# MLP and gate layers of a convolution-gated network as four interleaved 512-token lanes, with weight gradients as 22 PSUM jobs

## The chip, the cores and the metric

The kernel runs on 1 core of one Trainium2 chip. The metric is the device time of one execution in microseconds. One core has TensorE (PE, with a queue PEld for loading weights), VectorE (DVE), ScalarE (ACT), GpSimd (POOL) and SyncE (SP), which here only issues transfers; 16 DMA engines move data between DRAM, the on-chip memory SBUF and, through the engines, the accumulators in PSUM.

## What is computed

The reference is a forward pass of four residual layers over 2048 tokens of width 512, and all its gradients:

```python
def _A_ref(q, k, v, shift_k, ssm_k, ssm_D):      # gate layer
    kv = k_shift * v                             # k_shift: 4-tap causal shift convolution of k
    y = irfft(rfft(kv, 2 * S) * rfft(ssm_k, 2 * S))[:S] + kv * ssm_D
    return q * y
def _B_ref(x, w1, b1, w2, b2):                   # MLP, 512 -> 1376 -> 512
    return gelu(x @ w1 + b1) @ w2 + b2
x = A_q
x = x + _A_ref(_layernorm(x), A_k, A_v, A_shift_k, A_ssm_k, A_ssm_D)
x = x + _B_ref(_layernorm(x), B_w1, B_b1, B_w2, B_b2)
x = x + _A_ref(_layernorm(x), ...)               # the same weights again
x = x + _B_ref(_layernorm(x), ...)
_out, _vjp = jax.vjp(_f, A_q, ..., B_b2)
return (_out, *_vjp(grad_out))                   # x and ten gradients
```

Layers are numbered 0 and 2 (gate) and 1 and 3 (MLP). y is the same in both gate layers, so the convolution runs once forward and once backward.

## The kernel before

Tiles are 128 partitions wide: 2048 tokens are 16 token tiles, 512 features are 4 chunks, 1376 hidden features are 11 chunks, the last of them 96 wide. The program is a row of phases, each of which runs after the one ahead as far as its data and its memory allow.

`phase_conv_forward` does the transforms as matmuls; its last inverse matmuls are at L206, and y stays in SBUF. Then `load_weights` loads w1 (512 x 1376), w2 (1376 x 512) and the biases; w1 and w2 go through the ACT queue, b1 as single elements at L560 and L563 through SP.

`phase_forward` runs `a_layer_fwd` and `b_layer_fwd` twice. A gate layer takes LayerNorm statistics (L532, L534, a square root on ACT at L535), normalizes, multiplies with y and adds. An MLP layer normalizes all 16 token tiles (L625), transposes them on PE (L630, evicted at L631), and then, for each slice of 512 tokens and each of 11 chunks, multiplies with w1 into PSUM (L640), evicts with the bias (L643), and forms gelu and its derivative gp on pieces of 128 x 512: eight operations on DVE (L646 to L664) and two on ACT (L653, L659). gp is stored feature-major by POOL (L665). Four token tiles are then multiplied with w2 (L670); DVE and whichever engine is free add the residual and b2 (L673, L674); h is transposed on PE to token-major (L602, evicted at L604) and stored (L678).

`phase_backward` first transposes w1 and w2 on PE (`build_bwd_weights`, L716). `b_layer_bwd` transposes the gradient (L783), multiplies with w2T (L802), multiplies with gp (L804, which also sums the bias gradient), multiplies with w1T (L811), goes back through LayerNorm (L735 on) and stores gz token-major after PE transposes (L820). The weight gradients follow inside the same layer function. dW2 is formed in two groups of up to six PSUM accumulators; for each group all 16 token tiles of h are read again (L837) and multiplied (L839). dW1 has 12 accumulators in two groups, and reads gz (L865) and n (L867) again for each (L869). Layer 3's sums go to DRAM as 32-bit partials and are added to layer 1's. `a_layer_bwd` handles the gate layers.

`phase_conv_backward` begins at L967. It multiplies with PE at L994, loads kv and its transform matrix, and runs the same transforms again; its code is not touched by the change.

Each engine and each DMA queue executes its instructions in program order; a scheduler sets that order when the program is built, within the order of the phases.

## Time and profile before

| | us |
|---|---|
| runs | 1800.83, 1804.43, 1805.06 |
| median of the runs | 1804.43 |
| span of the profiled execution | 1812.6 |
| last inverse matmul of the forward convolution starts | 375.9 |
| last output matmul of the forward layers starts | 772.8 |
| last weight-gradient matmul starts | 1341.8 |

The profile is of one execution, whose span is 8.2 us over the median of the runs. Rows are quoted further down. A row of the timeline is one instruction: start, duration, engine, line of the program, operation, output and input tiles, shapes. A row of the windows gives each engine's busy time in a stretch of the span.

### The profile page before, as it was taken

The page shows a single profiled execution, that of the slowest core. Times are in us where ns is not written, and L with a number is a line of the kernel's source. Part 1 is how long each engine was busy: PE and PEld are TensorE (multiplying, and loading weights), DVE is VectorE, ACT ScalarE, POOL GpSimd, SP SyncE. Part 2 cuts the span into 40 slices and gives each one's busy share as a digit, 9 for nine tenths or more (in the row PEclk, how much of TensorE's full clock was granted, in tenths as well). Part 3 has the DMA queues.
Part 4 walks back from the last instruction along what each step waited for, and adds up shares of the span by engine and source line. Part 5 has one row for each costly group of instructions (what it writes and reads, how often), then busy time and mean ns, then how long its engine had stood idle before and what let it go on. Part 6 is the DMA issues. An engine that isn't in the chain of part 4 may idle for free.

```text
span 1812.6 us, 17191 instructions
## 1 busy us (share of the span) xinstructions
PE 1106.2 (61%) x5093; PEld 466.0 (26%) x5093; DVE 1148.1 (63%) x2935; ACT 670.2 (37%) x1122; POOL 335.1 (18%) x503
## 2 busy tenths in 40 slices
PE   4365950935777376749964669954656827642077
PEld 2022320412232132325521225411212302210033
DVE  8489716257999799926766007758213159999841
ACT  7433620138787777734314014301001302211321
POOL 0055200212222322200000000100000005554000
PEclk9687875965998599869987889988876958875588
DMA  5656474031212222263276754297875152121201
GB/s 49 233 184 203 157 285 172 0 79 71 77 72 103 84 75 75 88 205 126 91 251 196 232 176 138 94 189 219 273 221 204 47 221 70 58 61 43 62 14 47
DMA packets 128782, 237.64 MB, mean 131 GB/s; under 512 B 21919, under 2 KB 91579, under 8 KB 128048
## 3 DMA queue, kind: packets, MB, share of 16 engines
q1 hardware_dynamic: 81040, 117.24, 22.6%
q0 software_dynamic: 23168, 94.72, 13.8%
q10 hardware_dynamic: 24480, 24.58, 4.4%
q8 instruction: 40, 0.66, 0.2%
q14 instruction: 54, 0.44, 0.1%
HBM read 145.96 MB, written 90.52 MB: 130 GB/s over the span
## 4 chain that ended last, share of the span: by engine, by line
issue 46%; DVE 18%; DMA 13%; PE 11%; POOL 7%; SPq 3%; ACT 2%; another core or an unknown queue 1%; POOLq 0%; DVEq 0%; ACTq 0%
DMA dw_n<-n_d 4%; PE dw_ps L869 2%; DVE gwacc L1091 2%; DVE gk_tmp L1082 2%; POOL gp_d L665 2%; SPq L306 2%; DMA KVspec_d<-KVspec 2%; DMA kj<-in_A_k_dram 2%; PE fwd_psc L182 2%; PE fwd_pss L185 2%; DVE gk_acc L1083 1%; PE inv_A L198 1%; PE inv_A L200 1%; DMA out_dram<-gw_b 1%
## 5 line engine op out<-in xcount | busy, mean ns | idle before, releaser
L670 PE MATMUL o_ps<-w_sb,hT_sl 128*128 128x512 bf16 (+1 forms) x352 | 109.3, 415 | 62.8 <-DVE hT_sl L654 61.4
L869 PE MATMUL dw_ps<-gz_tm,dw_n 128*128 128x512 bf16 (+1 forms) x384 | 96.6, 399 | 75.8 <-DMA dw_n<-n_d 64.0
L839 PE MATMUL dw_ps<-g_bf,h_tm 128*128 128x512 bf16 (+1 forms) x352 | 101.3, 438 | 54.3 <-DMA h_tm<-htm_d 49.6
L640 PE MATMUL z_ps<-nT,w_sb 128*128 128x512 bf16 (+1 forms) x352 | 103.2, 417 | 10.0 <-ACT g_u L643 4.7
L802 PE MATMUL gh_ps<-gT,w2T 128*128 128x512 bf16 (+1 forms) x352 | 86.9, 384 | 2.0 <-DVE gzT_sl L804 2.0
L811 PE MATMUL gn_ps<-w1T,gzT_sl 128*128 128x512 bf16 (+1 forms) x352 | 83.6, 379 | 0.0
L665 POOL DMA_DIRECT2D gp_d<-g_gp x88 | 48.1, 547 | 162.6 <-DVE g_gp L664 138.0
L804 DVE SCALAR_TENSOR_TENSOR gzT_sl<-gh_ps,gp_sl 128x512 bf16<-128x512 f32 (+1 forms) x88 | 60.4, 689 | 25.6 <-PE gh_ps L802 25.3
L869 PEld LDWEIGHTS <-dw_n 128*128 128x128 bf16 x384 | 36.5, 106 | 136.0 <-DMA dw_n<-n_d 57.0
L670 PEld LDWEIGHTS <-hT_sl 128*128 128x128 bf16 (+1 forms) x352 | 35.7, 103 | 133.6 <-DVE hT_sl L654 97.1
L630 PE MATMUL tr_ps<-ident,b_n 128*128 128x128 bf16 x128 | 18.1, 291 | 80.9 <-ACT b_n L625 67.5
L1090 POOL TENSOR_TENSOR gw_prod<-sh_bf,k_t 128x512 bf16<-128x512 bf16 x48 | 58.9, 1228 | 43.9 <-DVE gwacc L1091 31.4
L653 ACT ACTIVATE g_s<-g_arg 128x512 bf16<-128x512 bf16 (+1 forms) x88 | 54.9, 625 | 31.8 <-DVE g_arg L651 31.3
L839 PEld LDWEIGHTS <-h_tm 128*128 128x128 bf16 (+1 forms) x352 | 35.9, 112 | 119.3 <-DMA h_tm<-htm_d 71.6
L198 PE MATMUL inv_A<-KVspec,Iblk 128*128 128x512 bf16 x64 | 25.5, 399 | 64.1 <-DVE KVspec L262 64.1
L659 ACT ACTIVATE g_oms<-g_s,onescol_f 128x512 bf16<-128x512 bf16 (+1 forms) x88 | 63.2, 720 | 2.2
L643 ACT ACTIVATE g_u<-z_ps,b1col 128x512 bf16<-128x512 f32 (+1 forms) x88 | 60.0, 683 | 7.6 <-DVE g_w L657 1.2
L1091 DVE TENSOR_TENSOR gwacc<-gwacc,gw_prod 128x512 f32<-128x512 f32 x64 | 60.8, 961 | 1.0 <-POOL gw_prod L1090 1.0
L747 ACT ACTIVATE lb_j<-agn 128x512 bf16<-128x512 bf16 x32 | 20.1, 627 | 111.3 <-DVE agn L898 92.0
L820 POOL DMA_DIRECT2D gztm_d<-gz_tmj x32 | 17.3, 541 | 235.3 <-ACT gz_tmj L604 231.0
L786 DVE TENSOR_TENSOR b2acc<-b2acc,b_ps 1x512 f32<-1x512 f32 x2 | 1.4, 675 | 93.5 <-PE b_ps L785 93.5
L1013 ACT ACTIVATE GYspec<-fwd_psc 128x512 bf16<-128x512 f32 x16 | 9.6, 598 | 136.0 <-PE fwd_psc L182 136.0
(300 smaller groups left out, 3004.3 us busy)
## 6 DMA issues: line engine op xcount, KB each, us to landing
h_tm<-htm_d SPq DMA_DIRECT2D x64, 344.0 KB, 4.2
gz_tm<-gztm_d SPq DMA_DIRECT2D x64, 344.0 KB, 3.9
htm_d<-h_tm POOLq DMA_DIRECT2D x32, 344.0 KB, 2.5
gztm_d<-gz_tmj POOLq DMA_DIRECT2D x32, 344.0 KB, 2.9
gp_d<-g_gp POOLq DMA_DIRECT2D x80, 128.0 KB, 2.1
gp_sl<-gp_d ACTq DMA_DIRECT2D x8, 1280.0 KB, 8.8
sst<-Hspec_d SPq DMA_DIRECT2D x64, 128.0 KB, 2.2
dw_n<-n_d SPq DMA_DIRECT2D x64, 128.0 KB, 3.7
```

Source lines behind the costliest of these rows:

```text
L640: nc.tensor.matmul(ps[0:fcs, :], lhsT=w.w1[:, dc, f0:f0 + fcs], rhs=nT[:, dc, cols], start=(dc == 0), stop=(dc == ND - 1))
L643: nc.scalar.activation(out=u[0:fcs], in_=ps[0:fcs], func=ACT.Identity, bias=w.b1col[0:fcs, c:c + 1], scale=1.0)
L659: nc.scalar.activation(out=oms[0:fcs], in_=sg[0:fcs], func=ACT.Identity, scale=-1.0, bias=consts.onescol_f[0:fcs, :])
L665: nc.gpsimd.dma_start(out=gp_dram[f0:f0 + fcs, cols], in_=gp[0:fcs])
L670: nc.tensor.matmul(ps2, lhsT=hT_sl[0:fcs, c, ti * P:(ti + 1) * P], rhs=w.w2[0:fcs, c, :], start=(c == 0), stop=(c == NFC - 1))
L802: nc.tensor.matmul(ps[0:fcs, :], lhsT=bw.w2T[:, dc, f0:f0 + fcs], rhs=gT[:, dc, cols], start=(dc == 0), stop=(dc == ND - 1))
L804: nc.vector.scalar_tensor_tensor(out=gzT_sl[0:fcs, c, :], in0=ps[0:fcs], scalar=1.0, in1=gp_sl[0:fcs, c, :], op0=ALU.mult, op1=ALU.mult, a ...
L811: nc.tensor.matmul(ps2, lhsT=gzT_sl[0:fcs, c, ti * P:(ti + 1) * P], rhs=bw.w1T[0:fcs, c, :], start=(c == 0), stop=(c == NFC - 1))
L839: nc.tensor.matmul(accs[c][0:fcs, :], lhsT=hm[:, f0:f0 + fcs], rhs=g_bf[:, t, :], start=(t == 0), stop=(t == NT - 1))
L869: nc.tensor.matmul(accs[(dc, fs0)][:, 0:fsz], lhsT=n_t[:, dc * P:(dc + 1) * P], rhs=gm[:, fs0:fs0 + fsz], start=(t == 0), stop=(t == NT - 1))
L1090: nc.gpsimd.tensor_tensor(out=prod, in0=sh[jj], in1=kt, op=ALU.mult)
L1091: nc.vector.tensor_tensor(out=gwacc[:, jj, :], in0=gwacc[:, jj, :], in1=prod, op=ALU.add)
```

## The change

The convolution phases stay. Everything between them is one new phase, `phase_mlp`.

The 2048 tokens are four lanes of 512. Each lane is a generator that walks through layers 0 to 3 (and in the backward pass 3 to 0) and yields estimated costs; `interleave` always resumes the lane whose clock is lowest, with the lanes started 12 (forward) or 8 (backward) units apart. A lane's x stays in SBUF as one 128 x 4 x 512 tile. LayerNorm's reciprocal root is a power on POOL. Transposes of n and of the gradients are DMA transposes (`turn`) instead of PE transposes. gelu runs on groups of up to four chunks, 128 x 2048: three ACT passes, two tensor_scalar and five tensor_tensor on DVE per group. Residual and b2 are added by PE as two more matmuls into the same accumulator, and ACT evicts. h, gp and gz are stored feature-major; the token-major copies are gone. All transfers of the phase are issued by SP.

In the backward pass the mean part of LayerNorm's gradient is taken out of w1T once, on DVE, when the weights are loaded (L551 to L553), and the other part is a matmul with a diagonal matrix built on POOL (L711, L713).

The weight gradients come after both layers: 22 jobs, 11 chunks of dW2 from h and 11 of dW1 from gz. A job brings in its chunk of both layers with two DMA transposes of 128 x 2048 (L779), multiplies 32 times into one accumulator (L784), and stores; dW1's results are transposed by DMA first (L792).

w1T and w2T are now made by DMA transposes from DRAM when the weights are loaded, before the forward pass (L541, L547). The last 96 columns of w1 come at L543: there the compiled program has, for each of the four row blocks, a plain transfer of 96 x 128 single elements.

The core of the diff, without the unchanged parts of formulas (removed functions are those shown above):

```diff
-    with tc.tile_pool(name="wsmall", bufs=1) as wsmall:
-        res.w = load_weights(nc, tc, wpool, wsmall, dims, aps)
-    phase_forward(nc, tc, dims, consts, dram, res, aps, dbg)
...
-    phase_backward(nc, tc, dims, consts, dram, res, aps, dbg)
+    with ExitStack() as res.gystack:
+        phase_mlp(nc, tc, dims, consts, dram, res, aps)
...
 def load_weights
+    w1_ap, w2_ap = aps["B_w1"], aps["B_w2"]
+    w.w1 = wpool.tile([P, ND, FP], BF16, name="w1_sb")
+    nc.sync.dma_start(out=w.w1[:, :, 0:F], in_=w1_ap.rearrange("(c p) f -> p c f", p=P))
...
+    for dc in range(ND):
+        rows = w1_ap[dc * P:(dc + 1) * P, :]
+        nc.sync.dma_start_transpose(out=w.w1T[:, 0:nfull, dc * P:(dc + 1) * P], in_=rows[:, 0:nfull * P])
+        if nfull < NFC:
+            nc.sync.dma_start_transpose(out=w.w1T[0:F - nfull * P, nfull, dc * P:(dc + 1) * P],
+                                        in_=rows[:, nfull * P:F])
+    for f0 in range(0, F, 512):
+        fsz = min(512, F - f0)
+        nc.sync.dma_start_transpose(out=w.w2T[:, :, f0:f0 + fsz], in_=w2_ap[f0:f0 + fsz, :])
...
+    for c in range(NFC):
+        st = small.tile([P, 6], F32, name="w1st", tag="w1st", bufs=3)
+        nc.vector.bn_stats(out=st, in_=w.w1T[:, c, :])
+        nc.vector.bn_aggr(out=mv[:, c, :], in_=st)
+        nc.vector.tensor_scalar(out=w.w1T[:, c, :], in0=w.w1T[:, c, :], scalar1=mv[:, c, 0:1], scalar2=None,
+                                op0=ALU.subtract)
...
 new functions
+def interleave(lanes):
+    clock = [off for off, _ in lanes]
+    gens = [g for _, g in lanes]
+    alive = set(range(len(gens)))
+    while alive:
+        i = min(alive, key=lambda k: (clock[k], k))
+        try:
+            clock[i] += next(gens[i])
+        except StopIteration:
+            alive.discard(i)
...
+def turn(nc, m, dst, src):
+    for t in range(TS):
+        nc.sync.dma_start_transpose(out=dst[:, :, t * P:(t + 1) * P], in_=src[:, t, :])
...
+    nc.scalar.activation(out=q, in_=zb, func=ACT.Square)
+    nc.vector.tensor_scalar(out=t, in0=q, scalar1=C_GELU2 * A_GELU, scalar2=C_GELU2, op0=ALU.mult, op1=ALU.add)
+    nc.vector.tensor_tensor(out=t, in0=t, in1=zb, op=ALU.mult)
+    nc.scalar.activation(out=sg, in_=t, func=ACT.Sigmoid)
+    nc.scalar.activation(out=o, in_=t, func=ACT.Sigmoid, scale=-1.0)
+    nc.vector.tensor_scalar(out=q, in0=q, scalar1=3.0 * C_GELU2 * A_GELU, scalar2=C_GELU2, op0=ALU.mult,
+                            op1=ALU.add)
+    nc.vector.tensor_tensor(out=h, in0=sg, in1=zb, op=ALU.mult)
+    nc.vector.tensor_tensor(out=o, in0=o, in1=h, op=ALU.mult)
+    nc.vector.tensor_tensor(out=o, in0=o, in1=q, op=ALU.mult)
+    nc.vector.tensor_tensor(out=gp, in0=o, in1=sg, op=ALU.add)
...
 b_fwd, per lane
+            nc.scalar.activation(out=zb[:, c - c0, :], in_=ps, func=ACT.Identity, bias=w.b1col[:, c:c + 1])
...
+        nc.sync.dma_start(out=m.h_d[l][:, c0:c0 + k, s * 512:(s + 1) * 512], in_=h[:, c0:c0 + k, :])
+        nc.sync.dma_start(out=m.gp_d[l][:, c0:c0 + k, s * 512:(s + 1) * 512], in_=gp[:, 0:k, :])
...
+        nc.tensor.matmul(ps, lhsT=m.ident, rhs=x[:, t, :], start=True, stop=False)
+        nc.tensor.matmul(ps, lhsT=w.ones_row, rhs=w.b2row, start=False, stop=False)
+        for c in range(NFC):
+            nc.tensor.matmul(ps, lhsT=h[:, c, t * P:(t + 1) * P], rhs=w.w2[:, c, :], start=False,
+                             stop=(c == NFC - 1))
+        nc.scalar.activation(out=x[:, t, :], in_=ps, func=ACT.Identity)
...
 b_bwd, per lane
+    gT = m.spool.tile([P, ND, 512], BF16, name="gT_sl", tag="nT", bufs=3)
+    turn(nc, m, gT, g)
+    n = m.spool.tile([P, TS, D], BF16, name="nb_sl", tag="n", bufs=m.n_bufs)
+    nc.sync.dma_start(out=n, in_=tok(m.n_d[l], s))
...
+            nc.vector.scalar_tensor_tensor(out=gz[:, c, :], in0=ps, scalar=1.0, in1=gp[:, c - c0, :], op0=ALU.mult,
+                                           op1=ALU.mult, accum_out=m.b1part[:, m.li[l], s, c:c + 1])
+        nc.sync.dma_start(out=m.gz_d[l][:, c0:c0 + k, s * 512:(s + 1) * 512], in_=gz[:, c0:c0 + k, :])
...
+        nc.gpsimd.tensor_scalar(out=dg, in0=m.ident, scalar1=cols[:, 0, t:t + 1], scalar2=-1.0 / D,
+                                op0=ALU.mult, op1=ALU.mult)
+        nc.tensor.matmul(ps, lhsT=dg, rhs=n[:, t, :], start=False, stop=True, skip_group_check=True)
+        nc.vector.scalar_tensor_tensor(out=go[:, t, :], in0=ps, scalar=m.rstd[l][:, s * TS + t:s * TS + t + 1],
+                                       in1=g[:, t, :], op0=ALU.mult, op1=ALU.add, accum_out=cols[:, 1, t:t + 1])
...
 weight_grads
+        for i, l in ((0, 3), (1, 1)):
+            nc.sync.dma_start(out=nres[:, i, :, :], in_=m.n_d[l].rearrange("(t p) d -> p t d", p=P))
...
+        for which in range(2):
+            for c, (f0, fcs) in enumerate(dims.FC):
+                src = m.h_d if which == 0 else m.gz_d
+                tm = tp.tile([P, 2, NT, P], BF16, name="dw_tm", tag="dw_tm")
+                for i, l in ((0, 3), (1, 1)):
+                    nc.sync.dma_start_transpose(out=tm[:, i, :, :], in_=src[l][:, c, :])
+                ps = pp.tile([P, D], F32, name="dw_ps", tag="dw_ps")
+                for i in range(2):
+                    for t in range(NT):
+                        rhs = m.G[i][:, t, :] if which == 0 else nres[:, i, t, :]
+                        nc.tensor.matmul(ps, lhsT=tm[:, i, t, :], rhs=rhs, start=(i == 0 and t == 0),
+                                         stop=(i == 1 and t == NT - 1))
+                o = evp.tile([P, D], BF16, name="dw_o", tag="dw_o")
+                nc.scalar.activation(out=o, in_=ps, func=ACT.Identity)
+                if which == 0:
+                    nc.sync.dma_start(out=out9[f0:f0 + fcs, :], in_=o[0:fcs, :])
+                else:
+                    oT = evp.tile([P, ND, P], BF16, name="dw_oT", tag="dw_oT")
+                    nc.sync.dma_start_transpose(out=oT, in_=o)
+                    nc.sync.dma_start(out=out7[:, f0:f0 + fcs].rearrange("(c p) f -> p c f", p=P),
+                                      in_=oT[:, :, 0:fcs])
...
 phase_mlp
+                nc.sync.dma_start(out=x, in_=tok(q_ap, s))
+                for l in (0, 2):
+                    yield from a_fwd(nc, m, x, l, s)
+                    yield from b_fwd(nc, m, x, l + 1, s)
+                nc.sync.dma_start(out=tok(out0, s), in_=x)
...
+        nc.sync.dma_start(out=G3, in_=go_ap.rearrange("(t p) d -> p t d", p=P))
...
+                yield from b_bwd(nc, m, G3[:, s * TS:(s + 1) * TS, :], 3, s, ret)
+                g, sg = ret.pop()
+                yield from a_bwd(nc, m, g, sg, 2, s, G1[:, s * TS:(s + 1) * TS, :], True, ret)
+                ret.pop()
+                yield from b_bwd(nc, m, G1[:, s * TS:(s + 1) * TS, :], 1, s, ret)
+                g, sg = ret.pop()
+                yield from a_bwd(nc, m, g, sg, 0, s, None, False, ret)
+                nc.sync.dma_start(out=tok(out1, s), in_=ret.pop())
+
+            interleave([(s * 8.0, bwd(s)) for s in range(NSL)])
```

Three places show how the instructions move. On SP, the queue from the end of the forward convolution to the gradient's load: before, the biases, the output and the gradient (w1 and w2 are on ACT's queue), then the reloads of h:

```order
L567 DMA b2t<-in_B_b_dram 128x512
L560 DMA b1t<-in_B_b_dram 128x10x1
L563 DMA b1t<-in_B_b_dram 96x1
L710 DMA out_dram<-x_4950 128x16x512
L929 DMA g_bf<-in_grad_out_dram 128x16x512
L837 DMA h_tm<-htm_d 128x1376 x32
```

Now the same queue, up to the first lane's data:

```order
L541 DMA_TRANSPOSE w1T_sb<-in_B_w_dram 128x10x128
L543 DMA w1T_sb<-in_B_w_dram 96x128x1
L541 DMA_TRANSPOSE w1T_sb<-in_B_w_dram 128x10x128
L543 DMA w1T_sb<-in_B_w_dram 96x128x1
L527 DMA w_sb<-in_B_w_dram 128x4x1376
L529 DMA w_sb<-in_B_w_dram 128x10x512
L538 DMA w_sb<-in_B_w_dram 96x512
L541 DMA_TRANSPOSE w1T_sb<-in_B_w_dram 128x10x128
L543 DMA w1T_sb<-in_B_w_dram 96x128x1
L541 DMA_TRANSPOSE w1T_sb<-in_B_w_dram 128x10x128
L543 DMA w1T_sb<-in_B_w_dram 96x128x1
```

All weight loads and the transposes have come into SP's queue, ahead of x (`L827`, four transfers). On DVE, the end of the weights' preparation in the changed kernel (w1st and w1mv are the statistics of w1T, ln_st those of the first lane's x):

```order
L551 BN_STATS w1st<-w1T_sb 128x6
L553 TENSOR_SCALAR w1T_sb<-w1T_sb,w1mv 128x512
L552 BN_AGGR w1mv<-w1st 128x2
L564 CAST b1col<-b1t 128x11
L584 BN_STATS ln_st<-x_sl 128x6
L553 TENSOR_SCALAR w1T_sb<-w1T_sb,w1mv 128x512
L585 BN_AGGR ln_mv<-ln_st 128x2
```

The first LayerNorm row (L584) stands behind all eleven statistics of w1T. On PE, the first dW2 job, before (a different accumulator for each chunk of a token tile):

```order
L839 LDWEIGHTS h_tm
L839 MATMUL dw_ps_8154<-g_bf,h_tm 128x512
L839 LDWEIGHTS h_tm
L839 MATMUL dw_ps_8155<-g_bf,h_tm 128x512
L839 LDWEIGHTS h_tm
L839 MATMUL dw_ps_8156<-g_bf,h_tm 128x512
```

and now (one accumulator for all token tiles of a chunk, G_4604 being the gradient of one layer):

```order
L784 LDWEIGHTS dw_tm
L784 MATMUL dw_ps<-G_4604,dw_tm 128x512
L784 LDWEIGHTS dw_tm
L784 MATMUL dw_ps<-G_4604,dw_tm 128x512
L784 LDWEIGHTS dw_tm
L784 MATMUL dw_ps<-G_4604,dw_tm 128x512
```

The loop over chunks has moved outside the loop over token tiles, and each chunk's operand comes from its own two transposes.

## Rows read from the trace of the kernel before

**Rows 1.** The page's first lines: span, then busy time by engine.
```profile
span 1812.6 us, 17191 instructions
...
PE 1106.2 (61%) x5093; PEld 466.0 (26%) x5093; DVE 1148.1 (63%) x2935; ACT 670.2 (37%) x1122; POOL 335.1 (18%) x503
```

**Rows 2.** Lines L206, L670, L869: durations min/median/max in ns, first and last start.
```profile
L206 PE MATMUL inv_A<-KVspec,Iblk x64: 379/379/379, 320.0 to 375.9; 128*128 128x512 bf16 x64
L670 PE MATMUL o_ps<-w_sb,hT_sl x352: 377/379/634, 444.8 to 772.8; 128*128 128x512 bf16 x160, 96*128 96x512 bf16 x16
L869 PE MATMUL dw_ps<-gz_tm,dw_n x384: 309/379/634, 995.8 to 1341.8; 128*128 128x512 bf16 x128, 128*128 128x352 bf16 x64
```

**Rows 3.** Busy time in windows, cut at stage ends; columns in the first line.
```profile
core 0: us, PE busy (x) PEld busy (x) DVE busy (x) ACT busy (x) POOL busy (x), PEclk, DMA share, GB/s
389.00:773.00 384.00, 237.39 (x1181) 103.05 (x1182) 353.18 (x1175) 299.81 (x494) 99.64 (x183) 0.83 0.22 80
773.00:1342.00 569.00, 403.44 (x2044) 179.85 (x2042) 276.83 (x758) 138.76 (x307) 39.44 (x73) 0.86 0.61 187
1186.00:1342.00 156.00, 89.59 (x332) 31.96 (x332) 67.90 (x163) 9.39 (x26) 9.19 (x17) 0.81 0.82 234
```

**Rows 4.** Costliest groups: busy us, mean ns, then idle before and its releaser.
```profile
L869 PE MATMUL dw_ps<-gz_tm,dw_n 128*128 128x512 bf16 (+1 forms) x384 | 96.6, 399 | 75.8 <-DMA dw_n<-n_d 64.0
L839 PE MATMUL dw_ps<-g_bf,h_tm 128*128 128x512 bf16 (+1 forms) x352 | 101.3, 438 | 54.3 <-DMA h_tm<-htm_d 49.6
L804 DVE SCALAR_TENSOR_TENSOR gzT_sl<-gh_ps,gp_sl 128x512 bf16<-128x512 f32 (+1 forms) x88 | 60.4, 689 | 25.6 <-PE gh_ps L802 25.3
```

**Rows 5.** Timeline of SP's queue: start us, duration us, instruction; two stretches.
```profile
1.25 0.84 SPq L303 DMA_DIRECT2D WT_d<-in_A_shift_k_dram  x1
2.14 33.79 SPq L306 DMA_DIRECT2D Dbc<-in_A_ssm_D_dram  x1
...
376.73 0.43 SPq L560 DMA_DIRECT2D b1t<-in_B_b_dram  x1
377.20 4.49 SPq L563 DMA_DIRECT2D b1t<-in_B_b_dram  x1
```

**Rows 6.** DMA issues: transfer, queue, count, KB each, median us from issue to landing.
```profile
h_tm<-htm_d SPq DMA_DIRECT2D x64, 344.0 KB, 4.2
...
gp_d<-g_gp POOLq DMA_DIRECT2D x80, 128.0 KB, 2.1
...
g_bf<-in_grad_out_dram SPq DMA_DIRECT2D x1, 2048.0 KB, 9.2
...
b1t<-in_B_b_dram SPq DMA_DIRECT2D x1, 2.5 KB, 11.7
...
out_dram<-gw_b SPq DMA_DIRECT2D x4, 1.0 KB, 6.4
```

**Rows 7.** Timeline of DVE: LayerNorm statistics, then gelu in the forward pass.
```profile
390.40 0.66 DVE L532 BATCH_NORM_STATS2 bnst<-x 128x6 f32<-128x512 bf16 x1
390.97 0.17 DVE L534 BATCH_NORM_AGGREGATE bnmv<-bnst 128x2 f32<-128x6 f32 x1
391.06 0.66 DVE L532 BATCH_NORM_STATS2 bnst<-x 128x6 f32<-128x512 bf16 x1
...
485.51 0.41 DVE L657 TENSOR_TENSOR g_w<-g_t,g_u 128x512 bf16<-128x512 bf16 x1
485.84 0.41 DVE L654 TENSOR_TENSOR hT_sl<-g_u,g_s 128x512 bf16<-128x512 bf16 x1
...
486.85 0.28 DVE L655 TENSOR_SCALAR g_t<-g_t 128x512 bf16<-128x512 bf16 x1
487.05 0.28 DVE L662 TENSOR_SCALAR g_arg<-g_arg 128x512 bf16<-128x512 bf16 x1
```

**Rows 8.** Timeline of ACT in the forward pass: z eviction and the two gelu passes.
```profile
480.97 0.69 ACT L643 ACTIVATE g_u<-z_ps,b1col 128x512 bf16<-128x512 f32 x1
481.56 0.62 ACT L653 ACTIVATE g_s<-g_arg 128x512 bf16<-128x512 bf16 x1
482.21 0.72 ACT L659 ACTIVATE g_oms<-g_s,onescol_f 128x512 bf16<-128x512 bf16 x1
```

**Rows 9.** Chain of waits in the forward convolution: start us, us, engine, eight matmuls.
```profile
205.43 1.73 PE fwd_psc L182 x8
```

More of the change, by code (lines that the diff above doesn't have):

```diff
@@ L518, in ssm_kernel @@
[L518 to L523 removed]
+        phase_conv_backward(nc, tc, dims, consts, dram, res, aps, dbg)
 C_GELU2 = 2.0 * math.sqrt(2.0 / math.pi)
 A_GELU = 0.044715
[L530 to L540 removed]
@@ new lines, in interleave, with a_fwd @@
+def interleave(lanes):
[8 more added lines that the diff above has]
+            alive.discard(i)
+def a_fwd(nc, m, x, l, s):
+    n = ln_slice(nc, m, x, l, s)
+    yield 4.0
+    yn = m.gpool.tile([P, TS, m.D], BF16, name="yn", tag="yn", bufs=1)
+    nc.vector.tensor_tensor(out=yn, in0=n, in1=m.y[:, s * TS:(s + 1) * TS, :], op=ALU.mult)
+    nc.vector.tensor_tensor(out=x, in0=yn, in1=x, op=ALU.add)
+    yield 3.0
```

617 lines of the change are left out of this document (208 added, 409 removed).

## Prediction

> **What bounds the kernel now.** I read the span first [rows 1]: 1812.6 us for the profiled execution, with DVE busy 63% of it and PE 61%; neither average bounds the whole. So I cut the span at stage ends, taken from the first and last start of one line [rows 2]: the last inverse transform of the forward convolution starts at 375.9, the last output matmul of the forward MLP at 772.8, the last weight-gradient matmul at 1341.8. The windows [rows 3] then show three regimes. From 389 to 773 DVE is busy 353.18 of 384 us: the forward is VectorE work, and PE (237.39) waits for it. From 773 to 1342 no engine is near full (PE 403.44 of 569). The two weight-gradient groups of the page [rows 4] say why: L839 lost 49.6 us to h_tm, L869 64.0 us to dw_n, both reloads from DRAM; in the last of these stretches, 1186 to 1342, the DMA share is 0.82 at 234 GB/s [rows 3], so that is a transfer stage. What follows 1342 is the backward convolution, 1812.6 - 1342 = 471 us, whose code is the same in both kernels. So 966 us, from 376 to 1342, are open to the change.
>
> **The change part by part**, against the profiled span; each term is a stage of the new kernel, the last sum is set beside the old one.
>
> *Stage 1, forward convolution:* code and order unchanged, 376 us [rows 2].
>
> *Stage 2, weights.* The old kernel loaded its weights during the convolution and had 13 us from the last inverse matmul to the first LayerNorm at 389. The new one cannot: its first SP transfer into w1T waits for the SBUF that y's last inverse matmul releases, and DVE's first LayerNorm row stands behind the eleven means over w1T (L551), which want all four quarters of w1T. Each quarter has a piece that is no hardware transpose: L543 reads 96 x 128 single elements of 2 bytes, 12,288 of them. The nearest row of the same kind is b1's load, also single elements into SBUF: after 128 x 10 = 1280 elements were issued (0.43 us) the queue took 4.49 us to give the next transfer [rows 5], that is 4.92 us / 1280 = 3.8 ns each, and 12,288 x 3.8 ns = 47 us. Four lie one behind the other on SP: 188 us. Bounds: a piece as cheap as any 128 KB load, 2.1 us [rows 6]; above, 6.9 ns (b1's 1280 elements landed after 11.7 us, 512 elements of gw_b after 6.4 us [rows 6]: 5.3 us / 768), 85 us a piece; far above, 16.5 ns from the start of the program (33.79 us behind 2048 elements that went from DRAM to DRAM [rows 5]), 203 us a piece. I take 3.8: same direction, same element, and the queue's own holding time; 11.7 us was measured beside other transfers. The rest of the stage: w1, w2 and the first x slices, 3.2 MB at 234 GB/s [rows 3], 14 us; the real transposes of w1 and w2, 2.6 MB, at the price chosen below for half a megabyte, 4.2 us, 22 us; 2 us until the first row starts. Together 226 us, so LayerNorm starts at 602 instead of 389. Nothing covers it: the MLP is the only work left, and the convolution's is done.
>
> *Stage 3, forward, 8 pairs of (gate, MLP) lane-layers.* Start to start, a tensor_tensor on 512 columns takes 0.33 us and a tensor_scalar 0.20 [rows 7]. If 0.07 us of each is a start that does not grow with the columns (what lies between the two lines through 0.33 and 0.20 at one and two columns a tick), I estimate for 2048 columns 1.135 and 0.60, for 1536 0.87 and 0.47. The five tensor_tensor of gelu over groups of 2048, 2048 and 1536 come to 15.7, its two tensor_scalar to 3.3; eight statistics pairs at 0.66 [rows 7] 5.3; n of the gate layer 1.3; its product and sum 2.3. That is 27.8 us of DVE, times 8: 222. ACT has 11 z evictions at 0.59, three gelu passes over 5632 columns at about 0.65 per 512 less starts, four n and four output evictions [rows 8]: 26, times 8, 208. PE has 96 matmuls per MLP lane-layer, 768 x 0.216 (1.73 / 8 [rows 9]) = 166. DVE still bounds. At the old occupancy, 353 / 384 = 0.92 [rows 3], 222 becomes 241; I add 15 to fill the lanes and 15 to empty the last one (52 matmuls are 11 us, and the evictions). 271 against 384. What was removed here: gelu's eight short DVE operations and its 512-column starts, the adds L673/L674, the transposes of h on PE and their ACT copies, now residual on PE and DMA transposes. The spills and the n transposes all stand on SP in order; a lane's transposes wait behind another lane's h and gp stores, which 12 clocks of offset are meant to cover: priced at nothing if they do, and in the third rival if not.
>
> *Stage 4, turn-round:* the gradient's load waits for the last output store: 9.2 us [rows 6], plus its transposes and the first gh, 16 us.
>
> *Stage 5, backward.* Each gz multiply is 0.69 (L804 [rows 4]); 11 of them, 8 more with accumulation in the MLP layer and 8 in the gate layer, two to three wide ones of 1.135: 21.2 us of DVE per pair, 170 in all; PE 736 x 0.216 = 159. DVE bounds again: 170 / 0.92 + 15 = 200.
>
> *Stage 6, weight gradients.* PE: 22 x 32 + 32 = 736 matmuls, 159 us if fed. The feeding is 44 DMA transposes of 512 KB from DRAM plus 4 MB of n. The old trace has no DMA transpose, so its price is bounded: below by a plain copy at 234 GB/s, 2.2 us [rows 3]; above by the element price applied to its 256-byte runs, 2048 x 3.8 ns = 7.8 us [rows 5]; I take 4.2 us, what the like-sized token-major load h_tm of 344 KB needed from issue to landing [rows 6]. 44 x 4.2 = 185, plus 18 for n at 234 GB/s: 203 us, DMA-bound. The old kernel reread h_tm, gz_tm and n 64 times each; those reads are gone.
>
> [...]
>
> *Stage 7, from the last weight-gradient matmul to the end:* 471 us as before; its first transfers still come after the last job's output on SP.
>
> Sum: 376 + 226 + 271 + 16 + 200 + 203 + 471 = 1763, against 1812.6. The profiled execution lies 8 us above the median of the runs, so **1755 us** against 1804.43. In short: the MLP itself gains some 260 us, and 213 of them go back in the prologue.
>
> **The rivals.**
> *Transposes at the price of a plain copy (2.2 us).* Stage 6 becomes PE-bound, 159 + 5 = 164, a gain of 39; the prologue's 2.6 MB gain 10: 1706. For it: 234 GB/s was held for 156 us [rows 3]. Against: runs of 256 bytes. [...]
> *Single elements cost nothing special (2.1 us a piece):* 4 x 45 = 180 less, 1575. For: it is only 24 KB. Against: both rows of single elements [rows 5]. [...]
> *Slower than before: the transposes cost their runs (7.8 us).* Place: 44 jobs' transfers in stage 6 and the weights in stage 2, with nothing beside them to do. 44 x 3.6 = 158 and 19: 1932. It decides the sign from 5.2 us per 512 KB on (49 half megabytes x 1.0 = 49 us, the whole gain).
> *Lanes don't fill:* the one SP queue and the rounds between ACT and DVE keep the forward at 384, +113: 1868. For: a transpose that waits on SP holds every lane's stores behind it. Against: three to four groups are in flight.
> *Elements at their landing price, 6.9 ns:* 4 x 38 = 152 more, 1907. *At 16.5 ns:* 4 x 156 = 624 more, 2379; the row is a write to DRAM, which L543 is not.
>
> **How the numbers follow.** Forecast 28%, with a range of its own of 1700 to 1820 (two of its stages off by a tenth or so). Plain-copy transposes 20%, cheap elements 12%, run-priced transposes 19%, unfilled lanes 9%, 6.9 ns 9%, 16.5 ns 3%. About 0.3% (1799 to 1810) is what a measurement of this kernel can tell from no change. Faster by more: 25 of the forecast's 28, with 20 and 12, is 0.57; within: 0.04; slower: 0.39. The range goes from 1575, the cheap-element case, to 1940, just over the run-priced one; outside lie half of the cheap-element case, 16.5 ns and the upper tails, under 2 in 10.
>
> **What would show it.** In the new profile: a stretch after the last inverse matmul, about 226 us long, with PE and DVE idle and L543 four times on SP, 40 to 50 us apart (right), or the first LayerNorm soon after 420 (cheap elements). Forward: DVE busy over 0.85 of some 270 us; below 0.65 the lanes don't fill. Weight gradients: PE waiting for dw_tm, transposes 4 to 5 us apart and the stage near 200 us; near 165 with PE at work throughout, the plain price; over 300, the run price. The tail from the last L784 matmul to the end must be 471 us; if it is not, a transfer that I took as unmoved has moved. The prediction fails most easily on two prices that no row of the old kernel carries: 12,288 single elements and 512 KB transposed.

## The result and the profile after

The changed kernel takes **1557.09 us** in the median (1553.35 to 1560.17) against 1802.63 us for the kernel before in the same comparison: a ratio of 0.8637, 95% interval 0.8618 to 0.8655. The forecast, 1755 us with a range of 1575 to 1940, had the sign right, but about a fifth of the gain, and the time lies 18 us below the range. The profiled execution has a span of 1558.4 us. These are the first lines of its page, which answer to [rows 1]; the last column of a group is its count:

```profile
span 1558.4 us, 12837 instructions
...
PE 989.9 (64%) x4028; PEld 403.3 (26%) x4109; DVE 920.9 (59%) x1840; ACT 503.9 (32%) x632; POOL 259.5 (17%) x369
```

Read in stages, as the forecast was made, the new span is cut by the first and last start of one line each (last inverse matmul 369.8, first LayerNorm 450.6, last eviction of x 709.6, first gh 727.9, first weight-gradient matmul, that of db2, 917.0, last weight-gradient matmul 1096.9):

| stage | forecast | measured | off by |
|---|---|---|---|
| 1 forward convolution | 376 | 369.8 | -6 |
| 2 weights, to the first LayerNorm | 226 | 80.8 | **-145** |
| 3 forward | 271 | 259.0 | -12 |
| 4 turn-round | 16 | 18.3 | +2 |
| 5 backward | 200 | 189.1 | -11 |
| 6 weight gradients | 203 | 179.9 | -23 |
| 7 the rest | 471 | 461.5 | -9 |
| sum | 1763 | 1558.4 | -205 |

The windows of the same stages, with the columns of [rows 3] (busy time and count by engine, granted clock as a share, DMA share, GB/s), for the weights, the forward, the backward and the weight gradients:

```profile
370.00:451.00 81.00, 0.91 (x3) 0.19 (x2) 13.66 (x44) 0.60 (x1) 0.11 (x1) 0.52 1.50 81
451.00:710.00 259.00, 194.18 (x753) 75.46 (x768) 228.69 (x345) 212.10 (x225) 40.66 (x64) 0.87 0.50 153
...
728.00:917.00 189.00, 166.62 (x722) 70.80 (x736) 151.97 (x432) 38.07 (x52) 23.66 (x60) 0.96 0.68 185
917.00:1097.00 180.00, 161.70 (x722) 72.02 (x735) 14.31 (x28) 15.47 (x25) 1.98 (x4) 0.94 0.89 186
```

The forward has shrunk from 384 us to 259 with DVE at 0.88 of it, and the weight gradients are at work on PE for 162 of 180 us. The 81 us in which no engine does anything to speak of are the price of the new way to load the weights; the forecast had 226 there, and that is where two thirds of its error lies. The next lines are SP's queue in that stretch (start, duration, instruction; a duration holds the time until the queue could go on):

```profile
370.27 1.47 SPq L541 DMA_TRANSPOSE w1T_sb<-in_B_w_dram  x1
371.79 0.56 SPq L543 DMA_DIRECT2D w1T_sb<-in_B_w_dram  x1
372.40 13.57 SPq L541 DMA_TRANSPOSE w1T_sb<-in_B_w_dram  x1
386.02 0.58 SPq L543 DMA_DIRECT2D w1T_sb<-in_B_w_dram  x1
386.78 13.10 SPq L527 DMA_DIRECT2D w_sb<-in_B_w_dram  x1
...
404.80 4.32 SPq L541 DMA_TRANSPOSE w1T_sb<-in_B_w_dram  x1
...
409.79 13.41 SPq L541 DMA_TRANSPOSE w1T_sb<-in_B_w_dram  x1
423.24 0.58 SPq L543 DMA_DIRECT2D w1T_sb<-in_B_w_dram  x1
423.86 20.78 SPq L547 DMA_TRANSPOSE w2T_sb<-in_B_w_dram  x3
444.74 0.53 SPq L559 DMA_DIRECT2D b1t<-in_B_b_dram  x1
445.31 1.03 SPq L562 DMA_DIRECT2D b1t<-in_B_b_dram  x1
```

What stands behind one of the first three pieces of single elements (L543) holds the queue about 13 us, where the first transpose, with nothing ahead of it, needs 1.47 and the third, behind plain loads, 4.32. The view of the DMA engines from 370 to 430 us, in 40 slices of 1.5 us (busy tenths, then GB/s), shows the same from the other end:

```profile
DMA  0989999999999999999999899999999999999999
GB/s 0 202 20 3 2 2 2 1 1 2 50 41 120 13 2 2 2 2 2 2 54 35 281 413 393 386 365 173 4 2 2 2 2 2 2 49 31 139 5 2
```

Busy engines that move 2 GB/s: single elements. So the piece is what the forecast took it for, and it does stand in the way; only its price is not 47 us. That row of b1 (L562) is the one on which the price rested: here the queue is held 1.03 us behind the same 1280 elements, where [rows 5] had 4.49.

### The profile page after: what moved, and what is told of

Its sections match the earlier page's. It is cut to its first block, busy times and chain, and to the rows that moved or that the text cites. A ratio compares the mean times of both kernels' runs of the same rounds, so it can differ in the third digit from the quotient of the medians.

```text
span 1558.4 us, 12837 instructions
## 1 busy us (share of the span) xinstructions
PE 989.9 (64%) x4028; PEld 403.3 (26%) x4109; DVE 920.9 (59%) x1840; ACT 503.9 (32%) x632; POOL 259.5 (17%) x369
## 4 chain that ended last, share of the span: by engine, by line
DVE 31%; PE 30%; DMA 15%; SPq 9%; issue 6%; ACT 5%; POOL 3%; another core or an unknown queue 1%; DVEq 0%; POOLq 0%; ACTq 0%
PE dw_ps L784 9%; PE fwd_psc L182 4%; PE fwd_pss L185 4%; DVE gwacc L995 3%; DVE gk_tmp L986 3%; DMA kj<-in_A_k_dram 2%; PE inv_A L198 2%; DMA KVspec_d<-KVspec 2%; SPq L541 2%; PE inv_A L200 2%; SPq L306 2%; PE gh_ps L694 2%; DMA sst<-Hspec_d 2%; PE inv_A L204 2%; PE inv_A L206 2%
## 5 line engine op out<-in xcount | busy, mean ns | idle before, releaser
L675 PE MATMUL o_ps<-w_sb,h_sl 128*128 128x512 bf16 x347 | 97.2, 422 | 32.6 <-DVE h_sl L644 32.1
L662 PE MATMUL z_ps<-nT_sl,w_sb 128*128 128x512 bf16 x342 | 83.1, 394 | 20.7 <-DMA nT_sl<-n_sl 14.4
L694 PE MATMUL gh_ps<-gT_sl,w2T_sb 128*128 128x512 bf16 x343 | 82.8, 387 | 20.5 <-DMA gT_sl<-G 19.5
L784 PEld LDWEIGHTS <-dw_tm 128*128 128x128 bf16 x704 | 69.1, 98 | 102.6 <-DMA dw_tm<-h_d 18.0
L784 PE MATMUL dw_ps<-G,dw_tm 128*128 128x512 bf16 x345 | 77.9, 386 | 17.9 <-DMA dw_tm<-h_d 17.5
L705 PE MATMUL gn_ps<-w1T_sb,gz_sl 128*128 128x512 bf16 x346 | 82.1, 383 | 0.2
L696 DVE SCALAR_TENSOR_TENSOR gz_sl<-gh_ps,gpb 128x512 bf16<-128x512 f32 x88 | 58.3, 688 | 30.5 <-PE gh_ps L694 26.6
L784 PE MATMUL dw_ps<-dw_n,dw_tm 128*128 128x512 bf16 x345 | 75.8, 379 | 0.4
L664 ACT ACTIVATE g_z<-z_ps,b1col 128x512 bf16<-128x512 f32 x88 | 54.5, 692 | 20.8 <-PE z_ps L662 13.2
L182 PE MATMUL fwd_psc<-P,Fblk 128*128 128x512 bf16 x124 | 40.2, 452 | 25.6 <-ACT h_b L336 16.3
```

The source lines that it names most:

```text
L182: nc.tensor.matmul(psc, lhsT=blocks(qc, a)[:, b * P:(b + 1) * P], rhs=inc[a], start=(a == 0), stop=(a == HT - 1))
L662: nc.tensor.matmul(ps, lhsT=w.w1[:, dc, c * P:(c + 1) * P], rhs=nT[:, dc, :], start=(dc == 0), stop=(dc == ND - 1))
L664: nc.scalar.activation(out=zb[:, c - c0, :], in_=ps, func=ACT.Identity, bias=w.b1col[:, c:c + 1])
L675: nc.tensor.matmul(ps, lhsT=h[:, c, t * P:(t + 1) * P], rhs=w.w2[:, c, :], start=False, stop=(c == NFC - 1))
L694: nc.tensor.matmul(ps, lhsT=w.w2T[:, dc, c * P:(c + 1) * P], rhs=gT[:, dc, :], start=(dc == 0), stop=(dc == ND - 1))
L696: nc.vector.scalar_tensor_tensor(out=gz[:, c, :], in0=ps, scalar=1.0, in1=gp[:, c - c0, :], op0=ALU.mult, op1=ALU.mult, accum_out=m.b1part ...
```

## The experiments

**What the four pieces cost.** The last 96 columns of w1, transposed out of the padded copy in SBUF instead:

```diff
-            nc.sync.dma_start_transpose(out=w.w1T[0:F - nfull * P, nfull, dc * P:(dc + 1) * P],
-                                        in_=rows[:, nfull * P:F])
+            nc.sync.dma_start_transpose(out=w.w1T[:, nfull, dc * P:(dc + 1) * P], in_=w.w1[:, dc, nfull * P:FP])
```

> The changed kernel, with the four pieces of 96 x 128 single elements (L543) replaced by four DMA transposes of 128 x 128 from the padded w1 in SBUF; nothing else. The trace of the changed kernel (span 1558.4) has stretches of 2 to 3 GB/s after each L543, and the next transfer on SP is held for 13.6, 13.1, 4.3 and 13.4 us, 53 for a transpose's landing. Theory A (single elements cost about 1.1 ns each, 13.5 us a piece): four pieces gone, 54 us less, 1503 us median. Theory B (the 13 us are a wait of a transpose for the plain transfer ahead, whatever its size): transposes still alternate with plain loads, so 15 us less at most, 1542. The forecast's price (3.8 ns) would be 188 us, which the stretch of 81 us no longer has room for.

Measured: 1518.06 us, ratio 0.8395 (0.8367 to 0.8423), span 1510.3. SP's queue in that run, where L542 is the new transpose:

```profile
370.92 4.84 SPq L540 DMA_TRANSPOSE w1T_sb<-in_B_w_dram  x3
...
383.69 3.69 SPq L542 DMA_TRANSPOSE w1T_sb<-w_sb  x3
...
390.11 6.22 SPq L545 DMA_TRANSPOSE w2T_sb<-in_B_w_dram  x3
396.43 0.53 SPq L557 DMA_DIRECT2D b1t<-in_B_b_dram  x1
```

From the first transpose to b1's load it is 25.5 us, against 74.5 in the changed kernel (370.27 to 444.74): the four pieces cost 49 us, 12.3 each, more than the four small transposes in their place (L542, 4.9 us of queue together), and the span is 48 us shorter: theory A, whose 54 was a little high. Theory B is out. The medians differ by 39 us, and by 44 when each is taken against the kernel before in its own comparison; runs of one kernel lie up to 12 us apart here.

**What their price goes by.** First half of the columns, so 48 partitions instead of 96; then half of the rows, so 64 elements in each partition instead of 128. Both have 6144 elements a piece, and leave the rest of this block of w1T at zero:

```diff
-            nc.sync.dma_start_transpose(out=w.w1T[0:F - nfull * P, nfull, dc * P:(dc + 1) * P],
-                                        in_=rows[:, nfull * P:F])
+            nc.sync.dma_start_transpose(out=w.w1T[0:48, nfull, dc * P:(dc + 1) * P],
+                                        in_=rows[:, nfull * P:nfull * P + 48])
...
+            nc.sync.dma_start_transpose(out=w.w1T[0:F - nfull * P, nfull, dc * P:dc * P + 64],
+                                        in_=rows[0:64, nfull * P:F])
```

> The changed kernel, with L543 reading 48 instead of 96 columns of w1, so 6144 single elements a piece instead of 12288; the columns left out are zero in w1T, so the gradient behind them lacks them. The number of transfers is unchanged; the order on SP has the four pieces and four transposes as before, three of each kind now behind one another. Theory A (price per element, 1.1 ns): 27 us less, 1530. Theory B (a price per transfer or per change between transposes and plain transfers): within 5 us of 1557, but for what the order gives.

> The changed kernel, with L543 reading 64 of the 128 rows of w1 in each piece: 96 partitions take 64 single elements each instead of 128, 6144 a piece, as many as in the run with 48 partitions; the part left out is zero in w1T, so the gradient behind it lacks it. The stretch from the first to the last weight transfer (first L541 to b1's load) was 74.5 us in the changed kernel, 25.5 without the pieces, 63.7 with 48 partitions of 128. Theory A (the elements of one partition go one behind the other, so a piece costs by its length per partition): half of the 49 us that the pieces cost goes, a stretch near 50, 1533 median. Theory B (a start per piece of about 7 us and 0.44 ns an element, as a line through the two runs gives): a stretch near 64, 1547, as with half of the partitions.

Measured: 1554.32 us (ratio 0.8604, 0.8575 to 0.8633) with half of the partitions, and 1539.32 (0.8517, 0.8501 to 0.8533) with half of the rows. The queue with half of the partitions, then with half of the rows:

```profile
374.24 4.63 SPq L541 DMA_TRANSPOSE w1T_sb<-in_B_w_dram  x3
...
383.95 22.71 SPq L543 DMA_DIRECT2D w1T_sb<-in_B_w_dram  x3
406.70 12.16 SPq L541 DMA_TRANSPOSE w1T_sb<-in_B_w_dram  x1
...
437.98 0.53 SPq L559 DMA_DIRECT2D b1t<-in_B_b_dram  x1
```

```profile
372.26 4.62 SPq L541 DMA_TRANSPOSE w1T_sb<-in_B_w_dram  x3
...
382.59 16.85 SPq L543 DMA_DIRECT2D w1T_sb<-in_B_w_dram  x3
399.49 7.80 SPq L541 DMA_TRANSPOSE w1T_sb<-in_B_w_dram  x1
...
419.77 0.53 SPq L559 DMA_DIRECT2D b1t<-in_B_b_dram  x1
```

The stretches are 63.7 and 47.5 us; less the 25.5 without the pieces, four pieces cost 38.2 and 22.0 instead of 49.0. Half of the partitions saved a fifth, half of the rows more than half. By its median the first of the two came out as its theory B, a price per transfer; the second, with as many transfers, is 18 us faster than the changed kernel, so that is out. So the price per element of the first run's theory A is wrong (it wanted 27 us from half of the elements and got 11 in the stretch), and so is the line with a start of 7 us that I drew after it. What fits all three is the length of one partition's row of elements: 12.3, 9.6 and 5.5 us over 128, 128 and 64 elements are 96, 75 and 86 ns for each step along it, whatever the number of partitions beside it, give or take a fifth. By the count they are 1.0, 1.6 and 0.9 ns an element, so it is the run with half of the partitions alone that speaks against the count. The view of the DMA engines gives the same times without a subtraction: stretches in which only elements move, at 1 to 2 GB/s in the mean, last about 12 us for one whole piece, 28 us for three with half of the partitions and 17 us for three with half of the rows. That does not tell whether the limit is on the side that reads rows of w1 or on the one that writes partitions; both were cut together in each run. Nor is the DMA share (the packets' time as a share of the engines) the same in these stretches: 1.78 in the changed kernel (374 to 383 us), 1.38 with half of the partitions (391 to 417) and 0.47 with half of the rows (389.5 to 405). What sets the pace stays open. b1 (128 partitions, 10 elements long) would be about 1 us by that, as the new traces have it.

**What a transpose costs, and what sets the weight-gradient stage.** A quarter of the matmuls, all transfers (the gradients of w1 and w2 then lack three of four token tiles):

```diff
-                    for t in range(NT):
+                    for t in range(0, NT, 4):
```

> The changed kernel, with 8 instead of 32 matmuls in each of the 22 weight-gradient jobs (three of four token tiles left out), all transfers as before. It prices the 512 KB transposes without PE. Theory A (about 2.7 us each in a row, as seven in 19.4 us on SP's queue in the changed kernel's trace): 44 x 2.7 + 18 for n = 137 us for the stage against 180, so 35 to 45 us less, 1515 to 1522. The forecast's 4.2 us: 203 us, no change from 1557. Plain-copy price 2.2 us: 115 us, 65 less, 1492.

Measured: 1537.62 us, ratio 0.8509 (0.8475 to 0.8544). From the first to the last L784 matmul it is 149 us (928.3 to 1077.2), against 171 in the changed kernel (925.5 to 1096.9). Three quarters of PE's work gone bring 22 us: the transfers were close behind. What PE waited for ahead of L784 in that run (us in total, times, longest):

```profile
PE dw_ps L784 <- DMA dw_tm<-h_d: 48.1, 15, 17.0
PE dw_ps L784 <- DMA dw_tm<-gz_d: 29.9, 21, 2.7
```

And one pair of gz's transposes on SP:

```profile
1057.81 0.53 SPq L793 DMA_DIRECT2D out_dram<-dw_oT  x1
1058.39 2.21 SPq L779 DMA_TRANSPOSE dw_tm<-gz_d  x1
1060.65 1.26 SPq L792 DMA_TRANSPOSE dw_oT<-dw_o  x1
1062.01 2.05 SPq L779 DMA_TRANSPOSE dw_tm<-gz_d  x1
```

A transpose of 512 KB holds the queue 1.8 to 2.9 us in the gz half of this run, 2.2 in the median (in the changed kernel 1.9 to 2.8, 2.2 in the median): the lower bound of the forecast, and not the 4.2 I took from h_tm. That 4.2 was a time from issue to landing, and as such it was good: in the changed kernel these transposes land 4.5 us after issue (median), but the next one goes out long before. With the small transposes and stores between, a gz job takes 6.1 us of queue (66.6 us for eleven) where its 32 matmuls take 6.9. So the gz half goes by PE, with the transfers 12% under it; what happens in the h half follows below. All three expectations missed: theory A's 137 us of transfers left out what SP issues between. The price is the first rival's: 2.2 us is what 512 KB takes at the 234 GB/s of [rows 3].

**Where PE's wait for the transposes comes from.** The loads of n moved behind the sixth and eighth job:

```diff
-        for i, l in ((0, 3), (1, 1)):
-            nc.sync.dma_start(out=nres[:, i, :, :], in_=m.n_d[l].rearrange("(t p) d -> p t d", p=P))
...
+                if which == 0 and c in (5, 7):
+                    i, l = ((0, 3), (1, 1))[(c - 5) // 2]
+                    nc.sync.dma_start(out=nres[:, i, :, :], in_=m.n_d[l].rearrange("(t p) d -> p t d", p=P))
```

> The changed kernel, with the two 2 MB loads of n (L765) issued after the sixth and eighth weight-gradient job instead of ahead of the first. In the changed kernel's trace PE waits 35.5 us in two stretches for h's transposes, 17.5 before the first job and the rest while the 4 MB of n stand ahead of the next transposes on SP. Theory A (the second wait is the place of the loads in the queue): 18 us less, 1539. Theory B (the DMA engines are full, share 0.92, and the bytes have to be moved anyway before the gz jobs): within 5 us of 1557.

Measured: 1555.06 us, ratio 0.8603 (0.8578 to 0.8629); its interval overlaps the changed kernel's. What PE waited for ahead of the same matmuls in the changed kernel, then in this run (L785 here):

```profile
PE dw_ps L784 <- DMA dw_tm<-h_d: 17.5, 1, 17.5
```

```profile
PE dw_ps L785 <- DMA dw_tm<-h_d: 10.8, 3, 5.9
```

The 35.5 us of the expectation count one stretch twice, 17.5 for PE and 18.0 for its weight loads: there is no wait of PE before the first job, only the one from 946.4 to 963.9, while the loads of n stand ahead of the transposes on SP. With the loads later it falls to 10.8 us, and the time from the first to the last of these matmuls from 171 to 164. Theory B is nearer: the transfers have to be moved anyway, and a better place in the queue gave 7 us in the stage and 2 in the median.

**Whether the lanes do anything.** The same lanes one behind the other:

```diff
-            interleave([(s * 12.0, fwd(s)) for s in range(NSL)])
+            interleave([(s * 1000.0, fwd(s)) for s in range(NSL)])
...
-            interleave([(s * 8.0, bwd(s)) for s in range(NSL)])
+            interleave([(s * 1000.0, bwd(s)) for s in range(NSL)])
```

> The changed kernel, with the lanes started 1000 units apart instead of 12 (forward) and 8 (backward), so that each lane's code stands whole behind the one ahead on every engine; the work is the same. Theory A (the interleaving fills DVE's waits): DVE's 229 us and PE's 194 of the forward no longer overlap fully; some 44 z matmuls and 52 output matmuls, 9.5 + 11 us, and the transposes' and LayerNorm's latency stand in the open in each of 8 lane-layers, about 8 x 10 = 80 us in the forward and half of that in the backward: 1640 to 1680. Theory B (the engines' own queues run ahead far enough, so order makes little difference): within 20 us of 1557.

Measured: 1716.00 us, ratio 0.9493 (0.9471 to 0.9516). Forward and backward, windows with the columns of [rows 3]:

```profile
458.00:806.00 348.00, 210.14 (x768) 78.39 (x768) 233.78 (x345) 215.89 (x225) 27.22 (x64) 0.77 0.35 115
...
822.00:1080.00 258.00, 175.97 (x735) 71.15 (x735) 158.91 (x434) 38.06 (x52) 27.14 (x59) 0.84 0.44 133
```

The same work on DVE (234 against 229 us) is spread over 348 us instead of 259, and the backward, from the first gh at 822.5 to the first db2 matmul at 1083.4, takes 261 instead of 189. Interleaving is worth 159 us: theory A by its mechanism, though its range ended 36 us short, since the backward loses nearly as much (72 us) as the forward (89) and not half of it.

**Whether the wide gelu operations do anything.** Groups of one chunk instead of four:

```diff
-        g.append((c, min(4, nfc - c)))
-        c += 4
+        g.append((c, 1))
+        c += 1
```

> The changed kernel, with groups of one chunk instead of four: gelu's operations on 128 x 512 instead of 128 x 2048, three to four times as many, and h, gp and gz stored and gp loaded in pieces of 128 KB. By the forecast's step (0.07 us of start in each DVE operation): 7 operations x 8 more starts x 8 lane-layers x 0.067 = 30 us more on DVE, which bounds the forward, 1587. Rival (SP bounds): 64 more stores of h and gp in the forward and 64 of gp and gz in the backward, 0.4 to 0.5 us of SP each, hold the transposes of n and of the gradient: 60 us more and above, 1620.

Measured: 1619.29 us, ratio 0.8963 (0.8945 to 0.8981). One group of DVE (busy us, mean ns of one, then idle before) in the changed kernel, and in this run; then this run's forward and backward:

```profile
L639 DVE TENSOR_TENSOR g_t<-g_t,g_z 128x2048 bf16<-128x2048 bf16 (+1 forms) x24 | 27.0, 1127 | 0.2
```

```profile
L639 DVE TENSOR_TENSOR g_t<-g_t,g_z 128x512 bf16<-128x512 bf16 x88 | 36.8, 418 | 1.0
```

```profile
453.00:754.00 301.00, 206.24 (x768) 74.74 (x768) 265.67 (x793) 235.94 (x419) 31.76 (x64) 0.82 0.41 134
770.00:975.00 205.00, 173.75 (x736) 71.84 (x737) 153.81 (x433) 38.07 (x52) 23.63 (x60) 0.95 0.61 173
```

DVE is busy 37 us longer in the forward (265.67 against 228.69), and the forward is 41 us longer (452.8 to 752.8): the start of each operation, 0.067 us in the forecast, is confirmed within a quarter (448 more operations, 30 us expected, 37 measured). The backward, where the groups only size transfers, is 16 us longer (205 against 189). Together they come to the rival's 1620, but not by the rival's way alone: most of it is DVE's. In the backward DVE's gz multiply (L696) waits 24.5 us for the loads of gp, against 3.2 in the changed kernel, which points to the transfers for the 16 us; whether SP's queue or the loads themselves cost them was not taken apart.

**The preparation of the weights beside the lanes.** w1's and w2's transposes and the eleven means become a generator of their own, started among the forward lanes; the pieces go through SBUF and n is loaded later, as above:

```diff
-            interleave([(s * 12.0, fwd(s)) for s in range(NSL)])
+            interleave([(s * 12.0, fwd(s)) for s in range(NSL)] +
+                       [(40.0, back_weights(nc, m.w, m.small, dims, aps))])
```

> The changed kernel with three edits: the four pieces as transposes from SBUF, the loads of n as in the run that moved them, and the transposes of w1 and w2 with the eleven means as a fifth generator beside the forward lanes, so that they no longer stand ahead of LayerNorm. Theory A (the weights' preparation is a stage by itself that nothing covers, and DVE has room for the means while lanes fill and empty): the first LayerNorm starts 20 us after the last inverse matmul instead of 81, DVE's 11 us of means lengthen the forward by up to 10, and 5 come from n: 1557 - 61 + 10 - 5 = 1501 median, below the 1518 of the run with the pieces alone. Theory B (SP's one queue is the limit in the forward pass: twelve more transposes ahead of the lanes' own hold them up): the forward gets longer by as much as the prologue gets shorter, no better than 1518.

Measured: 1515.48 us, ratio 0.8391 (0.8373 to 0.8408). The first LayerNorm starts at 379.7, 71 us earlier than in the changed kernel, but the run is no faster than the one with the pieces alone: theory B's outcome. The forward takes 287 us to the last eviction instead of 259. Its waits on DVE in the forward, then those of the changed kernel (us in total, times, longest):

```profile
DVE g_t L645 <- ACT g_q L644: 16.9, 7, 6.6
DVE h_sl L651 <- ACT g_s L647: 13.9, 7, 5.2
...
DVE w1st L572 <- DMA w1T_sb<-in_B_w_dram: 6.4, 1, 6.4
```

```profile
DVE g_t L638 <- ACT g_q L637: 6.1, 3, 2.3
DVE h_sl L644 <- ACT g_s L640: 5.6, 5, 1.5
```

The first of w1's transposes is now SP's first transfer of the phase, ahead of b1 and x, and the others stand there from 401 to 419 us, ahead of the first lane's stores:

```profile
373.06 1.46 SPq L560 DMA_TRANSPOSE w1T_sb<-in_B_w_dram  x1
```

So the scheduler had drawn the transposes to the front, where they were ready, and with them the first means: DVE waits 6.4 us for w1T at their head, and 31 instead of 12 for gelu's passes afterwards. To tell place from load, a last kernel holds the same preparation back until the last lane enters layer 3, by a small POOL copy of that lane's x into w1T and w2T, which the transposes then overwrite. Its code also stands behind the lanes now, and no longer among them:

```diff
                     yield from a_fwd(nc, m, x, l, s)
+                    if s == NSL - 1 and l == 2:
+                        for dc in range(ND):
+                            nc.gpsimd.tensor_copy(out=m.w.w1T[:, :, dc * P], in_=x[:, 0, 0:NFC])
+                        for f0 in range(0, F, 512):
+                            nc.gpsimd.tensor_copy(out=m.w.w2T[:, :, f0], in_=x[:, 0, 0:ND])
...
             interleave([(s * 12.0, fwd(s)) for s in range(NSL)])
+            for _ in back_weights(nc, m.w, m.small, dims, aps):
+                pass
```

> As the run with the weights behind the lanes, but a small POOL copy into w1T and w2T from the last lane's x, when it enters layer 3, makes the transposes and the means start at the end of the forward pass instead of at its beginning (the copied values are overwritten). Theory A (in the run before, the means on DVE and the transposes on SP cut into the start of the forward, where DVE waited 6.4 us for w1T and 31 instead of 12 for gelu's ACT passes): the forward is again near 260 from the first LayerNorm, the prologue stays at 7 us after the last inverse matmul, and the means go into the 18 us between the passes: 1515 - 25 = 1490 median. Theory B (the loads of w1, w2 and x themselves, now beside the first lanes, set the longer forward): no better than 1510.

> The changed kernel itself, unaltered, on the same chip as the run with the weights at the turn: 1557 us median if the runs of one kernel agree from chip to chip within 0.3%, and the stretch from the first L541 to b1's load again near 74 us.

Measured: **1492.26 us**, ratio 0.8260 (0.8242 to 0.8278), against 1564.17 and 0.8659 (0.8640 to 0.8677) for the changed kernel beside it. This is the fastest kernel of the study: 17% under the kernel before and 72 us under the changed one. Its windows from just before the first LayerNorm on: forward, turn-round, backward:

```profile
374.00:640.00 266.00, 190.88 (x756) 74.06 (x756) 234.05 (x377) 207.31 (x219) 44.24 (x71) 0.86 0.58 170
640.00:665.00 25.00, 5.12 (x15) 1.70 (x16) 4.57 (x6) 10.87 (x14) 0.00 (x0) 0.65 0.74 228
665.00:860.00 195.00, 172.86 (x763) 72.69 (x762) 159.15 (x447) 38.06 (x52) 23.55 (x60) 0.98 0.70 187
```

The first LayerNorm starts at 376.6, 6 us after the last inverse matmul (370.7), the last eviction of x is at 647.1, so the forward is 270.5 us with the means in it, and the first gh comes at 664.1, 17 us later, as before. The means were not pushed into the turn-round (they start between 581.0 and 618.6), but in the forward's last quarter they cost about 11 us and not 28. The copies and the new place of the code came together; what the place alone would have done was not tried. The changed kernel again needs 73.8 us from its first transpose to b1's load; its own median is 0.45% over that of the first comparison, the ratio 0.25%.

## Why the prediction was wrong

*What bounds the kernel, and the sign:* right. A forward bound by DVE and weight gradients bound by transfers were what the change went at.

*Stage 2, the step that failed:* the term "four pieces of 47 us" is 188 in the sum and 49 on the chip, 139 of the 205 us. The mechanism held: plain transfers of single elements, the next transfer on SP held behind each, LayerNorm behind the means of w1T, nothing to cover it. The size was off because the 4.49 us for which SP's queue was held behind b1's row [rows 5] were read as the price of its 1280 elements. The same row holds the queue 1.03 us in the changed kernel, 0.96 to 1.4 in the runs that leave it at its place, and 0.62 in the run with the weights at the turn, where b1 goes first. There its elements (1376 with the last 96) move by themselves, from 372.3 to 373.4 in the view from 371 to 375 us, whose 40 slices are 0.1 us each:

```profile
371.69 0.62 SPq L545 DMA_DIRECT2D b1t<-in_B_b_dram  x1
...
GB/s 0 0 0 0 0 0 0 0 0 0 0 0 0 2 2 1 1 3 3 3 2 2 3 3 85 83 133 103 102 92 164 195 215 246 266 328 348 256 246 266
```

That is 1.1 us, or 0.8 ns an element, at which a piece would take 10 us, near the 12.3 measured. So the hold is not the price of what stands ahead of it: for the same elements it was 4.49, 1.03 and 0.62 us. Why it was 4.49 in the kernel before is not shown. There the row stood beside other transfers (DMA share and GB/s at the end of the first line), but so it does in the changed kernel, behind w2's transposes (second line):

```profile
376.00:389.00 13.00, 0.98 (x4) 0.19 (x2) 2.35 (x6) 0.60 (x1) 0.11 (x1) 0.65 0.78 172
```

```profile
444.70:446.40 1.70, 0.00 (x0) 0.00 (x0) 0.00 (x0) 0.00 (x0) 0.00 (x0) 0.50 1.11 210
```

Whether the price goes by the count or by the length, b1 and a piece do not tell: 9.6 times the elements, 12.8 times the length and 11 times the time. That the price was 1 us could not be read from the old trace; that 4.49 might hold other transfers' time could have been, since the row stands in a busy stretch. I excused the landing time of 11.7 us with just that, "beside other transfers", and did not apply it to the queue's time two rows away.

*Stage 6:* the transposes were sized at 4.2 us each, and hold the queue for 2.2 in the median (seven in a row took 19.4 us, 2.8 each), so they were put at 1.5 to 1.9 times what they took: a time from issue to landing was put in for the time on the queue. So the stage is bound by PE for the most part, as the first rival had it, and not by DMA; with one wait of PE of 17.5 us it came to 180 instead of the rival's 164. 23 us of the error.

*Stages 3 and 5:* in the forward the sum was good: DVE's 222 us are 228.69, and what was high is what stood around them, 0.92 for occupancy and 15 us each to fill and to empty: 12 us. The step of 0.07 us with two slopes, an estimate from [rows 7] alone, fits: in the changed kernel, start to start, a tensor_tensor of gelu takes 1.13 us on 2048 columns and 0.87 on 1536, a tensor_scalar 0.60 and 0.47. From 512 columns on that is 0.52 and 0.26 ns a column, two to one. In the backward, 11 us shorter, I had DVE as the bound with 170 us; it has 152, and PE, with 167 instead of 159 and 0.88 busy, is the fuller engine.

*Stages 1 and 7:* 6 and 9 us less, with unchanged code. The end of the forward convolution starts its last matmul between 369.8 and 375.1 us in the eleven profiles of the changed kernel and its variants, none of which changes anything in it, and at 375.9 in the kernel before, so the 6 us are hardly more than scatter. The tail was 9 us shorter. From the last weight-gradient matmul to the load of the transform matrix it is 23.5 us in the kernel before (1341.8 to 1365.3) and 15.4 in the changed one (1096.9 to 1112.3), so 8 of the 9 us lie there; the old kernel's last partial sums (L879) and their stores stood in that stretch, ahead of the last loads of kv, but that was not tried.

*The rivals:* "cheap elements", 1575, came nearest, with a chance of 12%. Its reason was wrong as well: a piece is not as cheap as a 128 KB load (2.1 us), it is six times that. That it lands near is luck: stages 3, 5, 6 and 7 were each shorter than its sum had them. The range failed by ending at that case's middle, though two rivals pulling the same way, cheap elements and cheap transposes, had both been named: together they make 1755 - 180 - 49 = 1526, and the measured 1557 lies between that and 1575. Lanes that don't fill and prices on the other side (1868 to 2379) are out.
